# Seven query groups in the first round, four pixel chunks summed by GpSimd, and three more GELU chunks on VectorE

## The chip, the cores and the metric

The kernel runs on one core of a Trainium2 chip. The metric is the device time of one execution in microseconds; the kernel before takes 950.07 us, the median of three runs (949.9 to 951.19). Engines are named as in the profile: PE (TensorE, matmuls), ACT (ScalarE), DVE (VectorE), POOL (GpSimd), SP (SyncE, which here only issues transfers).

## The reference

Four batches of 12288 queries of 128 channels attend to keys that are made from pooled pixels; keys and values are the same matrix. What comes out goes through a two-layer network of width 2048.

```python
B, C, H, W = 4, 128, 384, 32                       # q: (B, H*W, C); kv: (B, H, W, C)
kv_pool = kv.reshape(B, H // 4, 4, W // 4, 4, C).mean(axis=(2, 4))
k = v = kv_pool.reshape(B, -1, C) @ w_sr           # 768 keys per batch
s = (q @ k.transpose(0, 2, 1)) / np.sqrt(C)
a = softmax(s)                                     # over the keys
x = (a @ v).reshape(B * H * W, C)
h = x @ w_in                                       # d_ff = 2048
out = (h * (1.0 / (1.0 + np.exp(-1.702 * h)))) @ w_out
```

## The kernel before

**Tiling.** A group is 512 queries; there are 96 groups, 24 a batch. For a group the scores are six chunks of 128 keys by 512 queries, and the network has 16 chunks of 128 hidden units by 512 tokens. A chunk is *filled* by one matmul of 512 columns into PSUM (L347 for scores, L593 for the network), taken by ACT with the exponential (L349) or GELU (L595) into one of 102 slots of the tile `ag`, and *drained* by matmuls from there: four of 129 columns for scores (L360: values and a column of ones for the sum), one of 512 for the network (L603). ACT takes one, two or three chunks in one instruction; PSUM has two areas of three banks for that, and the other banks serve sums of drains and small jobs (`acc`).

**Stages.** There are two rounds of 48 groups (batches 0 and 1, then 2 and 3): all scores of the round, then all of its network. At the start of the first round nothing is there, so the scores of the first six groups are taken key chunk by key chunk, as pixels land: `chunks` lists (group, key chunk), first groups 0 and 1 with two key chunks, then groups 2 to 5 with two, then each further key chunk for all six groups, then the remaining groups one by one.

**Keys of batches 0 and 1.** A pixel chunk is 128 partitions by 2048 numbers (16 pixels of 128 channels in a partition). `load_chunk` loads it with GpSimd's queue, casting float32 to bfloat16. `pool_chunk` sums four rows and four columns of pixels with 16 matmuls of 32 columns (L139: pixels as weights, `sum4` as the moving matrix), DVE copies the result (L142), `key_and_value` multiplies by `w_sr` both ways (L161, L162) and DVE copies keys and values (L163, L164). Batches 2 and 3 are summed by adding transfers, which the change leaves alone.

**Queries.** The first three query blocks (12 groups) are loaded by `load_q` and transposed on PE (`transpose_q`, L233); the others are cast to bfloat16 in DRAM by GpSimd's queue (`cast_q`) and brought in by a transposing transfer of SP's queue (`load_qT`). The attention's result is stored by `put_away` and brought back transposed by `bring_back`, both on SP's queue.

**What sets the order.** Each engine takes its instructions in the order in which the program is written. That order comes from a small model that runs while the program is built: `now` counts PE time in units of one 512-column matmul, `end` holds when ACT will be done with each instruction, `dve` when DVE will be done, `COST` and `COPY` what small jobs cost on PE and DVE. Fills go ahead of ACT by two; between them drains are put as long as the next fill is not held up; `extras` are small jobs that wait for a free spot, and `first` names jobs that stand ahead of a certain fill. `background(i)` starts loads and jobs when group i is first filled; `gate` makes GpSimd's queue wait until DVE has come to that place.

**Chunks that DVE takes.** DVE computes the exponential of 32 chunks and the GELU of some network chunks of the second round (`lent`, `lent_gelu`: 13 elementwise operations and two reciprocals), so that ACT has less to do. `RECIPROCAL` is the model's price of one such reciprocal.

Of the kernel before, what the change touches and what calls it, by code (L numbers as in the profile page):

```python
# [24 lines left out]
def kernel(  # L25
    ctx, tc, q, kv, w_sr, moe_w_in, moe_w_out, out,
):
    nc = tc.nc
    B, N, C = q.shape
    _, H, W, _ = kv.shape  # L30
    r = 4
    Hp, Wp = H // r, W // r
    J = Hp * Wp
    JC = J // 128
    d_ff = moe_w_in.shape[1]
    FCH = d_ff // 128
    scale = 1.0 / (C ** 0.5)
    G = 512
    SG = 4 * G
    NG = B * N // G  # L40
    NS = NG // 4
    GB = NG // B
# [10 lines left out]
    kv_r = kv.rearrange("b (ch p) (a w) c -> b a ch p (w c)", p=128, a=2)  # L53
# [6 lines left out]
    XS = NS // R  # L60
# [7 lines left out]
    kvtmp = ctx.enter_context(tc.tile_pool(name="kvtmp", bufs=1))  # L68
# [51 lines left out]
    def new_keys(b):  # L120
        kTs[b] = kvres.tile([128, J], BF, name="kT")

        vs[b] = kvres.tile([128, JC, C + 8], BF, name="v")
        nc.vector.memset(vs[b][:, :, C:C + 1], 1.0)

    def load_chunk(b, jc):

        a, ch = divmod(jc, HC)
        t = x_tile(XS - 1 - jc)
        nc.gpsimd.dma_start(out=t, in_=kv_r[b, a, ch])  # L130
        kv_tiles[b, jc] = t.rearrange("p (wp w1 c) -> p w1 wp c", w1=r, c=C)

    def pool_chunk(b, jc):
# [7 lines left out]
        pTs[b, jc] = kvtmp.tile([128, 128], BF, name="pTc", bufs=2)  # L141
        nc.vector.tensor_copy(pTs[b, jc], ps[:, 0:128])  # L142

    def key_chunk(b, jc):
        if jc == 0:
            new_keys(b)
        ps = acc()
        nc.tensor.matmul(ps[:, 0:128], w_sr_sb, pTs[b, jc], start=True, stop=True)
        nc.vector.tensor_copy(kTs[b][:, jc * 128:jc * 128 + 128], ps[:, 0:128])
# [5 lines left out]
        vs[b, jc] = True  # L155

    def key_and_value(b, jc):
        if (b, jc) == (1, 0):
            new_keys(b)
        ps = acc()  # L160
        nc.tensor.matmul(ps[:, 0:128], w_sr_sb, pTs[b, jc], start=True, stop=True)  # L161
        nc.tensor.matmul(ps[:, 128:256], pTs.pop((b, jc)), w_sr_sb, start=True, stop=True)  # L162
        nc.vector.tensor_copy(kTs[b][:, jc * 128:jc * 128 + 128], ps[:, 0:128])  # L163
        nc.vector.tensor_copy(vs[b][:, jc, 0:C], ps[:, 128:256])  # L164
        vs[b, jc] = True
# [55 lines left out]
    def load_q(s, lo, hi):  # L221
        nc.gpsimd.dma_start(  # L222
            out=qs[s].rearrange("p (g e) -> p g e", g=4)[:, lo:hi, :],
            in_=q_flat[s * SG + lo * G:s * SG + hi * G, :].rearrange("(g p i) c -> p g (i c)", p=128, i=4))
# [22 lines left out]
    load_chunk(0, 1)  # L247
    load_q(0, 2, 4)
    load_q(1, 0, 2)
    for jc in range(2, JC):  # L250
        load_chunk(0, jc)
    load_q(1, 2, 4)
    for s in range(2, QS):
        load_q(s, 0, 2)
        load_q(s, 2, 4)
    cast_q(3)
    cast_q(4)

# [67 lines left out]

    early = range(NG // R, NG // R + EARLY)
    rolling = [(i, JC - 1) for i in [*range(38, NG // R, 6), *range(57, 90, 6)]]
    lent = [(g, FCH - 1) for g in range(52, 94, 3)]
    aside = agpool.tile([128, K, 512], BF, name="aside")  # L330

    def weights(c):
# [161 lines left out]
    PART, FIRST = 24, 3  # L494

    def put_away(n, m):
        size = PART // 2 if n == 0 and m > FIRST + 1 else PART
        for o in range(m * PART, m * PART + PART, size):
            lo = n * XS * SG + o * T
            nc.sync.dma_start(out=x_bf[lo:lo + size * T, :].rearrange("(k p) c -> p k c", p=T),  # L500
                              in_=x[:, o * T:(o + size) * T].rearrange("p (k c) -> p k c", k=size))
# [22 lines left out]
    def background(i):  # L524

        first_round = i < GB * 2
        s = TURN.get(i, NS) if first_round else i // 4 + 3 if i % 4 == 0 else NS
        if s < NS:
            load_qT(s)
        if i in CAST:  # L530
            gate()
            for s in CAST[i]:
                cast_q(s)
        if i in (10, 12):
            gate()
            for jc in range(i % 10 * 3 // 2, i % 10 * 3 // 2 + 3):
                load_chunk(1, jc)
        if 0 <= i - 16 < JC:
            extras.append((key_and_value, 1, i - 16))
        if 0 <= i - 15 < JC:  # L540
            extras.append((pool_chunk, 1, i - 15))
        if i in (28, 33, 38):
            put_away(0, (i - 28) // 5)
        if i in (31, 36, 41):
            bring_back(0, (i - 31) // 5)
        if i == 27:
            gate()
# [98 lines left out]
    NA, NM = NG * JC, NG * FCH  # L646
    chunks, sizes = [], [1] * 2 + [2] * 28
    chunks += [(0, 0), (1, 0), (0, 1), (1, 1)]
    chunks += [(i, jc) for i in range(2, 6) for jc in range(2)]
    chunks += [(i, jc) for jc in range(2, JC) for i in range(6)]  # L650
    chunks += [(i, jc) for i in range(6, NG) for jc in range(JC) if i not in early and (i, jc) not in rolling]
    seq, todo = [], []
    todo_early = [("a", t, a) for t in range(NT) for a in range(2) if (t // TS * TS + TS - 1) // 4 in early]
    for n in range(R):
# [39 lines left out]
    def later(g):  # L694
        extras.append((transpose_q, g))

    def jobs(p):

        nonlocal now
        for f, *args in first.get(p, ()):  # L700
            if f in COST:
                now = max(now, free[next_acc()])
            f(*args)
            if f in COST:
                now += COST[f][0]
                free[last_acc] = copied(f)

    def prepare(p):

        nonlocal now  # L710
        kind, part = seq[p]
        for i, jc in part:
            if (kind, i) not in begun:
                begun.add((kind, i))
                (background if kind == "a" else background_moe)(i)
            while kind == "a" and ((key_and_value, i // GB, jc) in extras or (transpose_q, i) in extras):
                f, *args = extras.pop(0)
                now = max(now, free[next_acc()]) + COST[f][0]
                f(*args)
                free[last_acc] = copied(f)  # L720

    first = {
        0: [(pool_chunk, 0, 0), (transpose_q, 0), (warm, 1), (key_chunk, 0, 0), (transpose_q, 1)],
        1: [(value_chunk, 0, 0), (warm, 1)],
        2: [(pool_chunk, 0, 1), (warm, 2), (key_and_value, 0, 1), (warm, 1), (transpose_q, 2)],
        3: [(transpose_q, 3)],
        4: [(transpose_q, 4)],
        5: [(transpose_q, 5)],
        6: [(pool_chunk, 0, 2)],
        7: [(key_and_value, 0, 2)],  # L730
        9: [(pool_chunk, 0, 3)],
        10: [(key_and_value, 0, 3)],
        12: [(pool_chunk, 0, 4)],
        13: [(key_and_value, 0, 4)],
        15: [(pool_chunk, 0, 5)],
        16: [(key_and_value, 0, 5), (later, 6)],
        17: [(later, 7)],
        18: [(later, g) for g in range(8, 12)]}

    FIXED, CHUNK, SWITCH, HANDOVER, EVACUATE = 0.295, 1.978, 6.0, 1.0, 4.5
    COST = {pool_chunk: (1.9, 2.6), key_chunk: (0.3, 2.4), value_chunk: (0.3, 2.4),
            transpose_q: (1.05, 4.2), early_fill: (1.0, 5.5), key_and_value: (0.55, 3.5),
            transpose_pooled: (0.9, 3.6), make_k: (0.8, 3.2), make_v: (0.8, 3.7)}
    COPY = {pool_chunk: 1.5, key_chunk: 1.5, value_chunk: 1.5, key_and_value: 2.8, transpose_q: 3.2}
    SMALL = 0.26
    RECIPROCAL = 10.5
    PAUSE = 4.0  # L750
    end, extra_at = [], 0.0
    source, dve = None, 0.0
# [7 lines left out]
    def copied(f):  # L760
        if f not in COPY:
            return now + COST[f][1]
        on_dve(COPY[f])
        return max(now + COST[f][1], dve)

    def fill(p):
        nonlocal now
        if p >= len(seq):
            return
        kind, part = seq[p]  # L770
        prepare(p)
        if p == 4:
            turns.insert(0, 2)
        if p == narrow - 5:
            for m in (2, 5):
                turns.remove(m)
        if p == narrow:
            assert not any(m in closes for m in (2, 5))
            now = max(now, free.pop(2), free.pop(5))
        lo = K * (p % 2)  # L780
        (fill_attn if kind == "a" else fill_moe)(part, banks[:, lo:lo + len(part), :])
        if p >= 2:
            now = max(now, end[p - 2] + HANDOVER / 2)
        now += len(part)
        begin = max(now + HANDOVER / 2, end[p - 1] if p else 0.0)
        if p and kind != seq[p - 1][0]:
            begin += SWITCH
        end.append(begin + FIXED + CHUNK * len(part))
# [101 lines left out]
```

The softmax here doesn't subtract the row's maximum and nothing guards it: scores larger than these inputs give would overflow.

## Time and profile before

Busy time of the engines in the profiled execution, which spans 948.6 us:

| engine | busy us | instructions |
|---|---|---|
| PE | 941.8 | 6314 |
| ACT | 934.9 | 710 |
| DVE | 536.5 | 1035 |
| POOL | 66.5 | 114 |

| transfers | number | KB each | us from issue to landing (median) |
|---|---|---|---|
| pixels, GpSimd's queue (L130) | 11 | 512 | 10.4 |
| pixels, SP's queue (L242) | 1 | 1024 | 5.1 |
| queries for PE transposes (L222) | 5 and 2 | 256 and 128 | 15.5 and 5.5 |
| queries cast in DRAM (L209) | 21 | 512 | 6.9 |

ACT does 502 GELU instructions of three chunks, 8 of two; 162 exponentials of three chunks, 28 of two and 2 of one. The first exponential starts at 8.69 us; the third, which needs the second pixel chunk, at 12.28. A row of a group gives line, engine, operation, what is written and read, the count, then busy time and the mean duration, then the idle time of that engine just ahead and who ended it. Busy times of pipelined instructions overlap, so time between starts is what one costs.

### The profile page before, as it was taken

What the parts mean: (1) busy time and instruction counts of PE and PEld (TensorE: products, weight loads), DVE (VectorE), ACT (ScalarE), POOL (GpSimd) and SP (SyncE); (2) the same over time, 40 slices, a digit from 0 to 9 for tenths busy, and PEclk for the clock granted to TensorE, in tenths of its full rate; (3) what the DMA queues carried; (4) which work ended last, traced back from release to release, by engine and by line L of the source; (5) the groups of instructions that cost most, each with busy time, mean ns of one, the idle gap of its engine ahead of it and who ended that gap; (6) DMA issues with size and microseconds to landing.
All of it is one profiled execution on the core that took longest, in us unless ns stands there. A gap on an engine that the chain in (4) does not pass through costs nothing.

```text
span 948.6 us, 15423 instructions
## 1 busy us (share of the span) xinstructions
PE 941.8 (99%) x6314; PEld 502.9 (53%) x6314; DVE 536.5 (57%) x1035; ACT 934.9 (99%) x710; POOL 66.5 (7%) x114
## 2 busy tenths in 40 slices
PE   8999999999999999999999999999999999999998
PEld 4677776444444444454446777754444444444444
DVE  4643653102577777778655765365666665566631
ACT  6999999999999999999999999999999999999998
POOL 3101001320000232000000000000000000000000
PEclk9999999999999999999999999999999999999999
DMA  9999922999767799864335583562222222222222
GB/s 209 209 170 193 206 64 45 158 125 180 153 130 115 113 154 119 123 103 79 64 55 113 134 161 76 133 122 36 43 35 44 34 46 34 45 33 45 34 45 45
DMA packets 372855, 95.46 MB, mean 101 GB/s; under 512 B 346720, under 2 KB 370400, under 8 KB 372320
## 3 DMA queue, kind: packets, MB, share of 16 engines
q1 hardware_dynamic: 344000, 62.36, 36.9%
q0 software_dynamic: 28512, 31.99, 22.3%
q8 instruction: 49, 0.80, 0.4%
q14 instruction: 22, 0.18, 0.1%
q10 hardware_dynamic: 272, 0.13, 0.0%
HBM read 52.49 MB, written 48.76 MB: 107 GB/s over the span
## 4 chain that ended last, share of the span: by engine, by line
ACT 88%; PE 9%; DMA 2%; issue 0%; DVE 0%; POOL 0%; POOLq 0%
ACT ag L595 71%; ACT ag L349 17%; PE banks L347 4%; PE banks L360 3%; DMA qT<-q_bf 1%; DMA x<-in_kv_dram 1%; PE banks L139 0%; PE banks L593 0%; PE banks L631 0%; ACT L595 0%; PE banks L603 0%; PE banks L233 0%; ACT L349 0%; DVE kT L163 0%; POOL x L222 0%
## 5 line engine op out<-in xcount | busy, mean ns | idle before, releaser
L595 ACT ACTIVATE ag<-banks 128x1536 bf16<-128x1536 f32 (+1 forms) x510 | 682.2, 1507 | 0.0
L593 PE MATMUL banks<-x,w_in_sb 128*128 128x512 bf16 x1522 | 411.7, 379 | 0.1
L603 PE MATMUL banks<-ag,w_out_sb 128*128 128x512 bf16 x1506 | 407.8, 379 | 0.0
L349 ACT ACTIVATE ag<-banks 128x1536 bf16<-128x1536 f32 (+2 forms) x192 | 245.8, 1439 | 3.8 <-PE banks L347 3.4
L603 PEld LDWEIGHTS <-w_out_sb 128*128 128x128 bf16 x1520 | 148.4, 98 | 178.1 <-issue 0.9
L593 PEld LDWEIGHTS <-w_in_sb 128*128 128x128 bf16 x1522 | 147.3, 98 | 170.4 <-issue 1.1
L614 DVE STREAM_TRANSPOSE o_sb<-banks 128x512 f32<-128x512 f32 x95 | 67.9, 715 | 210.7 <-PE banks L603 195.0
L360 PEld LDWEIGHTS <-ag 128*128 128x128 bf16 x2272 | 146.1, 98 | 46.4 <-issue 0.6
L360 PE MATMUL banks<-v,ag 128*128 128x129 bf16 x2272 | 163.7, 220 | 0.1
L347 PE MATMUL banks<-qT,kT 128*128 128x512 bf16 x544 | 148.7, 379 | 1.6 <-DVE kT L163 1.0
L439 DVE SCALAR_TENSOR_TENSOR ea<-ea,eb 128x512 f32<-128x512 f32 x128 | 87.9, 687 | 3.2
L383 DVE RECIPROCAL rec<-banks 128x3 f32<-128x3 f32 x124 | 22.3, 180 | 95.9 <-PE banks L360 95.9
L386 DVE TENSOR_TENSOR x<-banks,rec 128x384 bf16<-128x384 f32 x124 | 69.1, 558 | 4.3
L347 PEld LDWEIGHTS <-kT 128*128 128x128 bf16 x544 | 46.3, 98 | 26.5 <-DVE kT L163 1.7
L470 DVE RECIPROCAL eb<-ea 128x256 f32<-128x256 f32 x28 | 47.6, 1727 | 0.5
L173 POOL DMA_DIRECT2D kvs<-in_kv_dram x32 | 40.4, 1299 | 17.8 <-DMA kvs<-in_kv_dram 15.2
L428 DVE TENSOR_SCALAR ea<-banks 128x512 f32<-128x512 f32 x32 | 22.1, 692 | 32.8 <-PE banks L412 32.5
L463 DVE SCALAR_TENSOR_TENSOR ea<-ea,eb 128x512 f32<-128x512 f32 x56 | 38.3, 685 | 1.6
L518 POOL MEMSET gate_tile<- 1x1 f32 x37 | 3.9, 105 | 326.6 <-DVE gate_tile L517 326.6
L434 DVE SCALAR_TENSOR_TENSOR eb<-eb,ea 128x512 f32<-128x512 f32 x32 | 22.1, 690 | 0.9
L450 DVE TENSOR_SCALAR qT<-banks 128x512 f32<-128x512 f32 x14 | 9.7, 692 | 17.2 <-PE banks L406 16.9
L441 DVE SCALAR_TENSOR_TENSOR ag<-ea,ee 128x512 bf16<-128x512 f32 x24 | 16.5, 688 | 0.7
(83 smaller groups left out, 267.9 us busy)
## 6 DMA issues: line engine op xcount, KB each, us to landing
out_dram<-o_sb SPq DMA_DIRECT2D x380, 64.0 KB, 2.0
kvs<-in_kv_dram POOLq DMA_DIRECT2D x32, 384.0 KB, 6.3
q_bf<-in_q_dram POOLq DMA_DIRECT2D x21, 512.0 KB, 6.9
x_bf<-x SPq DMA_DIRECT2D x13, 768.0 KB, 5.8
x<-in_kv_dram POOLq DMA_DIRECT2D x11, 512.0 KB, 10.4
x_bf<-x SPq DMA_DIRECT2D x6, 384.0 KB, 4.6
x<-in_q_dram POOLq DMA_DIRECT2D x5, 256.0 KB, 15.5
x<-in_kv_dram SPq DMA_DIRECT2D x1, 1024.0 KB, 5.1
```

The lines of the kernel that those rows point to most:

```text
L173: nc.gpsimd.dma_start(out=kv_sums[b][:, i2], in_=kv_p[b, i, w, :, i2], **({"accum_op": ADD} if n else {}))
L347: nc.tensor.matmul(ps[:, k, :], kTs[i // GB][:, jc * 128:(jc + 1) * 128], rhs, start=True, stop=True)
L349: nc.scalar.activation(place([("a",) + c for c in chunks]), ps, AF.Exp, scale=scale)
L360: nc.tensor.matmul(av_of[u][:, k * (C + 1):(k + 1) * (C + 1)], weights(("a", i, jc))[:, o:o + T], vs[i // GB][:, jc, 0:C + 1], start=(jc = ...
L386: nc.vector.tensor_tensor(to, ps[:, :, 0:C], rec.unsqueeze(2).broadcast_to([128, TS, C]), MUL)
L439: nc.vector.scalar_tensor_tensor(a, a, COEFFS[k], b, ADD, MUL)
L463: nc.vector.scalar_tensor_tensor(a, a, COEFFS[k], b, ADD, MUL)
L470: nc.vector.reciprocal(b[:, m:m + 256], a[:, m:m + 256])
L593: nc.tensor.matmul(ps[:, k, :], w_in_sb[:, fc * 128:(fc + 1) * 128], x[:, g % (4 * XS) * G:(g % (4 * XS) + 1) * G], start=True, stop=True)
L595: nc.scalar.activation(place([("m",) + c for c in chunks]), ps, AF.Gelu_apprx_sigmoid)
L603: nc.tensor.matmul(o_of[g], w_out_sb[:, fc, :], weights(("m", g, fc)), start=(fc == 0), stop=(fc == FCH - 1))
L614: nc.vector.transpose(o_sb, o_of.pop(g))
```

## The change

Five parts:

1. The first round takes seven groups key chunk by key chunk instead of six. Loads are reordered for it: half of block 1's second part comes ahead of pixel chunks 2 to 5, the other half behind. One warm-up matmul is dropped ahead of `transpose_q(2)`.
2. The model of the order gets landings (`LAND`, in its units) and times at which keys and queries are ready (`ready`), so that it knows when PE would stand and waits.
3. Of the second batch's six pixel chunks, four are loaded as float32 by SP's queue, two at a time into the same two places, and summed over the four columns by GpSimd (three adds each); two are cast by GpSimd's loads as before. Pooling and keys of this batch go in pairs of chunks.
4. `lent` has 17 chunks instead of 14, two and three groups apart in turn; `RECIPROCAL` falls from 10.5 to 8.2.
5. `put_away` of the first round stores in halves from its second part on, instead of its last ones alone.

The aim is less work for ACT (4), less for PE (3), and an order of the first round that stands less (1, 2).

```diff
+    SUMS = 4
+    held, sums = {}, {}
+
+    def load_pixels(jc):
+        a, ch = divmod(jc, HC)
+        o = (XS - 4 + jc % 2 * 2) * SG
+        t = x[:, o:o + 2 * SG].bitcast(F32)
+        if jc < 2:
+            nc.vector.memset(t[:, 0:1], 0.0)
+        nc.sync.dma_start(out=t, in_=kv_r[1, a, ch])
+        kv_tiles[1, jc] = t.rearrange("p (wp w1 c) -> p w1 wp c", w1=r, c=C)
+
+    def sum_pixels(jc):
+        t = kv_tiles.pop((1, jc))
+        if jc % 2 == 0:
+            held[jc // 2] = opool.tile([128, 512], F32, name="o_sb").bitcast(BF)
+        sums[jc] = held[jc // 2][:, jc % 2 * 512:jc % 2 * 512 + 512].rearrange("p (wp c) -> p wp c", c=C)
+        nc.gpsimd.tensor_tensor(t[:, 0], t[:, 0], t[:, 1], ADD)
+        nc.gpsimd.tensor_tensor(t[:, 2], t[:, 2], t[:, 3], ADD)
+        nc.gpsimd.tensor_tensor(sums[jc], t[:, 0], t[:, 2], ADD)
+
+    def pool_pair(b, jc):
+        ps = acc()
+        for k in range(2):
+            t = None if jc + k in sums else kv_tiles.pop((b, jc + k))
+            for wp in range(4):
+                o = k * 128 + 32 * wp
+                parts = [t[:, w, wp, :] for w in range(r)] if t is not None else [sums[jc + k][:, wp, :]]
+                for w, part in enumerate(parts):
+                    nc.tensor.matmul(ps[:, o:o + 32], part, sum4, start=(w == 0), stop=(w == len(parts) - 1))
+        pTs[b, jc] = kvtmp.tile([128, 256], BF, name="pTp")
+        nc.vector.tensor_copy(pTs[b, jc], ps[:, 0:256])
...
-    for jc in range(2, JC):
-        load_chunk(0, jc)
-    load_q(1, 2, 4)
-    for s in range(2, QS):
-        load_q(s, 0, 2)
-        load_q(s, 2, 4)
+    load_q(1, 2, 3)
+    load_chunk(0, 2)
+    load_chunk(0, 3)
+    load_chunk(0, 4)
+    load_chunk(0, 5)
+    load_q(1, 3, 4)
+    load_q(2, 0, 2)
+    load_q(2, 2, 4)
...
-    lent = [(g, FCH - 1) for g in range(52, 94, 3)]
+    lent = [(g, FCH - 1) for g in range(52, 94) if g % 5 in (2, 4)]
...
-        size = PART // 2 if n == 0 and m > FIRST + 1 else PART
+        size = PART // 2 if n == 0 and m > 0 else PART
...
-        if i in (10, 12):
+        if i == 10:
             gate()
-            for jc in range(i % 10 * 3 // 2, i % 10 * 3 // 2 + 3):
+            for jc in range(2):
+                load_pixels(jc)
+            for jc in range(SUMS, JC):
                 load_chunk(1, jc)
-        if 0 <= i - 16 < JC:
-            extras.append((key_and_value, 1, i - 16))
-        if 0 <= i - 15 < JC:
-            extras.append((pool_chunk, 1, i - 15))
+        if 0 <= i - 11 < SUMS:
+            sum_pixels(i - 11)
+            if i - 9 < SUMS:
+                load_pixels(i - 9)
+        for at_, jc in ((17, 0), (19, 4), (21, 2)):
+            if i == at_:
+                extras.append((pool_sums if jc < SUMS else pool_pair, 1, jc))
+            if i == at_ + 1:
+                extras.append((key_pair, 1, jc))
...
-    chunks += [(i, jc) for i in range(2, 6) for jc in range(2)]
-    chunks += [(i, jc) for jc in range(2, JC) for i in range(6)]
+    chunks += [(i, jc) for i in range(2, 7) for jc in range(2)]
+    chunks += [(i, jc) for jc in range(2, JC) for i in range(7)]
...
+        now = max(now, free[next_acc()], LAND.get((f, *args), 0.0), ready.get((f, *args), 0.0))
+        f(*args)
+        now += COST[f][0]
+        free[last_acc] = copied(f)
...
-        2: [(pool_chunk, 0, 1), (warm, 2), (key_and_value, 0, 1), (warm, 1), (transpose_q, 2)],
+        2: [(pool_chunk, 0, 1), (warm, 2), (key_and_value, 0, 1), (transpose_q, 2)],
...
-    RECIPROCAL = 10.5
+    RECIPROCAL = 8.2
...
+    LAND = {(transpose_q, 0): 0.9, (transpose_q, 1): 3.8, (pool_chunk, 0, 1): 15.1, (transpose_q, 2): 21.0, (transpose_q, 3): 21.0, (transpose_q, 4): 26.9, (transpose_q, 5): 26.9, (transpose_q, 6): 29.8, (pool_chunk, 0, 2): 41.1, (pool_chunk, 0, 3): 52.5, (pool_chunk, 0, 4): 67.5, (pool_chunk, 0, 5): 78.8, (transpose_q, 7): 81.7, (transpose_q, 8): 87.6, (transpose_q, 9): 87.6, (transpose_q, 10): 93.5, (transpose_q, 11): 93.5}
+    ready = {}
...
+        if kind == "a":
+            now = max(now, *[ready.get(("k", i // GB, jc), 0.0) for i, jc in part], *[ready.get(("q", i), 0.0) for i, jc in part])
```

The jobs that `first` names move by one fill accordingly: group 6's transpose stands ahead of fill 6, pooling and keys of pixel chunks 2 to 5 ahead of fills 7, 8, 10, 11, 14, 15, 17 and 18.

More of the change, by code (lines that the diff above doesn't have):

```diff
@@ L142, in pool_chunk, with pool_sums, key_pair @@
         nc.vector.tensor_copy(pTs[b, jc], ps[:, 0:128])
+    SUMS = 4
[27 more added lines that the diff above has]
+        nc.vector.tensor_copy(pTs[b, jc], ps[:, 0:256])
+    def pool_sums(b, jc):
+        pool_pair(b, jc)
+    def key_pair(b, jc):
+        if not any(k == (b, m) for k in vs for m in range(JC)):
+            new_keys(b)
+        ps = acc()
+        pT = pTs.pop((b, jc))
+        nc.tensor.matmul(ps[:, 0:256], w_sr_sb, pT, start=True, stop=True)
+        for k in range(2):
+            nc.tensor.matmul(ps[:, 256 + k * 128:384 + k * 128], pT[:, k * 128:(k + 1) * 128], w_sr_sb,
+                             start=True, stop=True)
+        nc.vector.tensor_copy(kTs[b][:, jc * 128:(jc + 2) * 128], ps[:, 0:256])
+        nc.vector.tensor_copy(vs[b][:, jc:jc + 2, 0:C], ps[:, 256:512].rearrange("p (k c) -> p k c", k=2))
+        vs[b, jc] = vs[b, jc + 1] = True
     def key_chunk(b, jc):
@@ L157, in key_and_value @@
     def key_and_value(b, jc):
-        if (b, jc) == (1, 0):
-            new_keys(b)
         ps = acc()
@@ L648 @@
     chunks += [(0, 0), (1, 0), (0, 1), (1, 1)]
-    chunks += [(i, jc) for i in range(2, 6) for jc in range(2)]
-    chunks += [(i, jc) for jc in range(2, JC) for i in range(6)]
-    chunks += [(i, jc) for i in range(6, NG) for jc in range(JC) if i not in early and (i, jc) not in rolling]
+    chunks += [(i, jc) for i in range(2, 7) for jc in range(2)]
+    chunks += [(i, jc) for jc in range(2, JC) for i in range(7)]
+    chunks += [(i, jc) for i in range(7, NG) for jc in range(JC) if i not in early and (i, jc) not in rolling]
     seq, todo = [], []
@@ L695, in later, with job @@
         extras.append((transpose_q, g))
+    def job(f, args):
+        nonlocal now
+        if f not in COST:
+            now += args[0] if f is warm else 0.0
+            f(*args)
+            return
+        now = max(now, free[next_acc()], LAND.get((f, *args), 0.0), ready.get((f, *args), 0.0))
+        f(*args)
+        now += COST[f][0]
+        free[last_acc] = copied(f)
+        if f is pool_chunk:
+            for then in (key_chunk, value_chunk, key_and_value):
+                ready[(then, *args)] = free[last_acc]
+        if f in (key_chunk, key_and_value):
+            ready[("k", *args)] = free[last_acc] - (1.0 if f is key_and_value else 0.0)
+        if f is transpose_q:
+            ready["q", args[0]] = free[last_acc]
     def jobs(p):
-        nonlocal now
         for f, *args in first.get(p, ()):
[L701 to L706, printed above, removed]
+            job(f, args)
     def prepare(p):
@@ L715, in prepare @@
                 (background if kind == "a" else background_moe)(i)
-            while kind == "a" and ((key_and_value, i // GB, jc) in extras or (transpose_q, i) in extras):
+            while kind == "a" and ((key_pair, i // GB, jc // 2 * 2) in extras or (transpose_q, i) in extras):
                 f, *args = extras.pop(0)
-                now = max(now, free[next_acc()]) + COST[f][0]
-                f(*args)
-                free[last_acc] = copied(f)
+                job(f, args)
     first = {
@@ L728 @@
         5: [(transpose_q, 5)],
[L729 to L738, printed above, removed]
+        6: [(transpose_q, 6)],
+        7: [(pool_chunk, 0, 2)],
+        8: [(key_and_value, 0, 2)],
+        10: [(pool_chunk, 0, 3)],
+        11: [(key_and_value, 0, 3)],
+        14: [(pool_chunk, 0, 4)],
+        15: [(key_and_value, 0, 4)],
+        17: [(pool_chunk, 0, 5)],
+        18: [(key_and_value, 0, 5), (later, 7)],
+        19: [(later, 8)],
+        20: [(later, 9), (later, 10), (later, 11)]}
     FIXED, CHUNK, SWITCH, HANDOVER, EVACUATE = 0.295, 1.978, 6.0, 1.0, 4.5
-    COST = {pool_chunk: (1.9, 2.6), key_chunk: (0.3, 2.4), value_chunk: (0.3, 2.4),
+    COST = {pool_chunk: (1.9, 2.6), pool_sums: (1.1, 3.2), pool_pair: (3.8, 3.2), key_pair: (1.1, 5.0), key_chunk: (0.3, 2.4), value_chunk: (0.3, 2.4),
             transpose_q: (1.05, 4.2), early_fill: (1.0, 5.5), key_and_value: (0.55, 3.5),
             transpose_pooled: (0.9, 3.6), make_k: (0.8, 3.2), make_v: (0.8, 3.7)}
-    COPY = {pool_chunk: 1.5, key_chunk: 1.5, value_chunk: 1.5, key_and_value: 2.8, transpose_q: 3.2}
+    COPY = {pool_chunk: 1.5, pool_sums: 2.1, pool_pair: 2.1, key_pair: 4.2, key_chunk: 1.5, value_chunk: 1.5, key_and_value: 2.8, transpose_q: 3.2}
     SMALL = 0.26
-    RECIPROCAL = 10.5
+    RECIPROCAL = 8.2
     PAUSE = 4.0
```

## Prediction

> **What bounds the kernel now.** I read the page first, then ACT's groups by form, then PE and ACT in order of time, then busy time by stage, then the waits.
>
> ```profile
> PE 941.8 (99%) x6314; PEld 502.9 (53%) x6314; DVE 536.5 (57%) x1035; ACT 934.9 (99%) x710; POOL 66.5 (7%) x114
> ...
> ACT 88%; PE 9%; DMA 2%; issue 0%; DVE 0%; POOL 0%; POOLq 0%
> ```
>
> Two engines are busy for 99%. The chain that ended last is ACT for 88%, but that alone does not say that PE has room, so I look at the stages (us of the window, then busy us of PE, weight loads, DVE, ACT, GpSimd).
>
> ```profile
> 12.28:38.00 25.72, 24.30 (x259) 15.19 (x257) 17.04 (x44) 25.55 (x28) 1.68 (x5) 1.00 1.09 211
> 38.00:142.00 104.00, 103.54 (x1220) 75.66 (x1219) 50.87 (x150) 103.45 (x78) 9.07 (x23) 1.00 0.88 163
> 142.00:487.00 345.00, 345.00 (x1820) 165.32 (x1818) 196.99 (x366) 344.99 (x257) 48.03 (x70) 1.00 0.78 116
> 604.00:936.00 332.00, 332.00 (x1663) 155.61 (x1662) 191.67 (x276) 331.97 (x248) 0.00 (x0) 1.00 0.29 48
> 936.00:948.60 12.60, 9.35 (x89) 5.88 (x87) 1.52 (x4) 7.99 (x10) 0.00 (x0) 1.00 0.32 59
> ```
>
> From 12.28 us on ACT is idle for some 0.8 us until 936. In 604 to 936 there are 1663 matmuls in 332 us, 0.200 us each, some nine in ten of them 512 wide; a 512-wide matmul starts some 0.214 us after the one ahead (in the timeline below, three of L347 from 52.51, the next operation at 53.15), so PE has no gap there either, and works off drains that lie behind. The two engines are balanced: the end comes from whichever has more left. A gain needs both to be shortened.
>
> ACT's price of one instruction in the last stage, and its only idle spots in the first:
>
> ```profile
> L595 ACT ACTIVATE ag<-banks 128x1536 bf16<-128x1536 f32 x246 | 330.8, 1480 | 0.0
> ```
>
> ```profile
> 12.28 88.65 ACT L349 ACTIVATE ag<-banks 128x1024 bf16<-128x1024 f32 x74 [2.30 <-PE banks L347]
> 101.36 29.78 ACT L349 ACTIVATE ag<-banks 128x1536 bf16<-128x1536 f32 x22 [0.42 <-PE banks L347]
> ```
>
> The first column of the group is the union: 330.8 / 246 = 1.345 us per instruction of three chunks; the mean of 1.480 overlaps. The wait of 2.30 us before 12.28 hangs on the landing of the second pixel chunk.
>
> PE around the second batch's pooling, and what PE waits for in the whole run:
>
> ```profile
> 52.10 0.55 PE L139 MATMUL banks<-sum,x 128*128 128x32 bf16 x16
> 52.51 0.81 PE L347 MATMUL banks<-qT,kT 128*128 128x512 bf16 x3
> ...
> 54.53 0.22 PE L162 MATMUL banks<-w_sr_sb,pTc 128*128 128x128 bf16 x1
> 54.86 0.67 PE L360 MATMUL banks<-v,ag 128*128 128x129 bf16 x9
> ```
>
> ```profile
> PE banks L347 <- DVE kT L163: 1.0, 4, 0.4
> ...
> PE banks L412 <- DMA qT<-q_bf: 0.4, 1, 0.4
> ```
>
> A pooled chunk holds PE 52.51 - 52.10 = 0.41 us for 16 matmuls (0.025 us each). After the first key matmuls of the batch PE stands from 54.53 to 54.86, 0.33 us where 0.06 would do.
>
> **What the Trainium skill says.** "Trainium Kernel Development and Optimization", Performance Expectations: matmul busy time is a bad metric, as matmuls are pipelined. The trace agrees (L347 shows a mean of 0.379 us a matmul, but starts are 0.214 apart), so I count PE by starts. "GPSIMD Engine Reference", 3.1: a float32 `tensor_tensor` add of 2048 columns took 4.497 us there; no GpSimd add is in this trace. "DMA: Bandwidth & Descriptors", Anatomy of one DMA: about 2.0 us plus bytes / 436e3, written for GpSimd's loads, so for 1 MB an estimate of 4.4 us; this trace's one 1024 KB pixel load, from SP, took 5.1 us beside others.
>
> **The change part by part.**
>
> *17 GELU chunks instead of 14 on DVE.* The second round's list falls from 754 to 751 chunks; eight two-chunk instructions stay at its end, so exactly one three-chunk instruction goes: ACT -1.345 us. PE still makes the same matmuls. DVE pays: a chunk has 8 operations of about 0.69, 5 of about 0.43 and two reciprocals of 1.727 us, so about 11.1 us busy and, with the transposes that come between, some 14 us from first to last. DVE's 191.67 us of 332 become 225, 68%. The chunks stand 2 and 3 groups apart instead of 3; a group takes about 6.85 us, so two jobs of 14 us have 34 us. They fit, with little room in the shorter gap: 0 to +0.4 us on PE if a group's drain has to wait.
>
> *Four chunks of the second batch summed on GpSimd, pooling and keys in pairs.* PE now: 6 x 0.41 = 2.46 us. After: a summed chunk takes 4 matmuls, not 16, so 4 x 0.10 + 2 x 0.41 = 1.22 us. PE -1.24. Keys in pairs: 256 + 2 x 128 columns for a pair, the same columns as before: 0. The stall of 0.27 us behind the first key is three operations of DVE before the copy; with half as many handovers I take it away: PE -0.27, and of ACT's late starts at 52.10, 56.21 and 60.46 (together 0.47 us over their 1.33 us beat) some 0.3. DVE copies the same columns in half the instructions: off the path.
>
> GpSimd: 512 columns of the page's add are an estimate of 4.497 / 4 = 1.1 us; low end the DVE row of 0.69 us, high end double, 2.3 us, for contention. Three adds, the third waiting on two: about 3.7 us a chunk, 15 in all. Is it in time? Group 10's background fires at 37.8 us (where GpSimd's gate stands now), and a group lasts two instructions of 1.33, 2.66 us. Two pixel loads of 1 MB and two casting loads share the queues (2.45 us per MB by today's landings, 45.47, 47.92, 50.39): first pixels in by 45, second by about 49. Sums done at 49 and 53; they are used by group 17's job, 37.8 + 7 x 2.66 = 56.4. Loads three and four wait for sums one and two, land by 53 and 57; sums at 57 and 61, used at group 21, 67. Spare 3 and 6 us. Behind the waiting adds in GpSimd's queue stand the casts of query blocks 6, 7 and 8 (46.72, 48.39 and 52.37 now): they go out at 53, 57 and 61 and take some 5; their transposes start at 65.35, 68.18 and 71.75. Hidden, but only just. Behind the waiting pixel loads in SP's queue nothing stands until 65.35. So 0.
>
> *First round with seven groups; loads in another order; one warm-up matmul less.* The second pixel chunk still lands at 9.80, since nothing ahead of it is moved, so ACT's start at 12.28 stays but for the dropped warm-up: the transposes ran at 11.42 behind it, the fill at 11.65, and the key copy (11.20 plus 0.3) would allow it at 11.5: -0.1 on both. Chunks three to six land about 0.6 us later (256 KB of queries go ahead), but each is needed 0.9 us later or more: the four waits on kT (1.0 us) stay, as the order of pool, key and fill around them is the same. The first drain needs the third pixel chunk for groups 0 and 1, one two-chunk instruction (0.905 us) later than now; PE has nothing else then, so it may lose 0.3 to 0.9 us, which a better view of landings may give back, since the writer of the order now knows when PE would stand. I take 0 net, range -1.0 to +0.9.
>
> *Smaller stores at put_away; RECIPROCAL 8.2.* The unit of the order is one matmul, so 8.2 is 1.77 us, close to the 1.727 measured; 10.5 was 2.27. It only lets DVE's jobs be put closer. Halved stores may let the query transpose that landed at 100.07 in sooner: ACT's late start there (0.55 us over its beat) halves or stays: ACT -0.2.
>
> **Sum.** ACT: -1.345 - 0.1 - 0.3 - 0.2 = -1.95. PE: -1.24 - 0.27 - 0.1, and 0.27 us at 936.44, where PE waits for ACT and which it need not any more: -1.9. So both get about 1.9 to 2.0 shorter: 950.07 - 1.95 = 948.1 us.
>
> **Rivals.** (a) PE becomes the bound: the first round's later drains cost the 0.3 to 0.9, the stall behind the first key comes back (0.27), the longer DVE jobs cost 0.2: PE gets -1.0 at most, 949.1, no change that can be told. For it: PE is full to the end already. Against it: the four kT waits have some slack to give. (b) GpSimd's adds take double, or DVE's accesses hold them up: sums of 7 us each end at 52, 59, 66 and 73, so PE stands some 2.5 us at 56.4 and up to 6 at 67, with ACT behind it; less the gain, 950.6 to 954, likely 952. For it: nothing in this trace shows the price. Against it: the margin at the page's price. (c) The denser GELU jobs finish late and hold the drains of their groups, 17 times 0.15 us: 950.6. Against it: DVE waits 106 us for o in that stage now. (d) The order with landings also removes the early stalls (ACT's late starts up to 142 us come to 1.9 us over the beat): -3.0, 947.0.
>
> **How the numbers follow.** Main case 0.40, (a) 0.27, (b) 0.12, (c) 0.07, (d) 0.14. Main and (d) are faster by over 0.2% (under 948.17), but the main case lies on the edge, so of its 0.40 I give 0.10 to no change; (a) is no change but for 0.05. Faster 0.46, same 0.34, slower 0.20. Range: (d) down to 946.6; up to 951.0, which leaves the worse half of (b) out.
>
> **What would show it.** L595 three-chunk instructions 501 instead of 502; ACT's first two-chunk instruction at about 12.2; the second batch's pooling with 48 matmuls instead of 96; GpSimd's adds near 1.1 us and done before the sums' matmuls, with no wait of PE on GpSimd; PE's waits on kT still about four. Wrong if PE waits for GpSimd, if gaps appear on PE in 604 to 936, or if the first drain moves by more than 1 us.

## The result, and the profile after

The changed kernel takes 957.11 us (median of six executions, 953.34 to 958.05) where the kernel before takes 950.28: a ratio of 1.0063, with a 95% interval of 1.0044 to 1.0081. It is slower by 6.8 us; 948.1 was predicted. The profiled execution, spanning 951.5 us, is the shortest of the six, and shows only part of the loss; the trace of a longer one stands among the experiments.

The page's busy times and the chain of the changed kernel:

```profile
PE 940.9 (99%) x6262; PEld 501.9 (53%) x6262; DVE 569.2 (60%) x1072; ACT 933.5 (98%) x709; POOL 79.3 (8%) x122
...
PE 54%; ACT 43%; DMA 2%; DVE 0%; issue 0%; POOL 0%; POOLq 0%
```

ACT has one instruction less (709). PE has 52 matmuls less (6262): 48 in the pooling, three in the keys taken in pairs, one warm-up, as the working had it. But the chain that ended last has gone over: it was ACT for 88%, now PE has more than half of it, and ACT's wait at the very end, for what PE still has to do, grew from 1.3 to 3.3 us. PE sets the end.

By stage (us of the window, then busy us of PE, weight loads, DVE, ACT, GpSimd, the granted clock):

```profile
100.00:104.00 4.00, 2.49 (x22) 1.55 (x23) 2.00 (x5) 1.38 (x2) 0.00 (x0) 1.00 0.87 190
604.00:936.00 332.00, 332.00 (x1679) 156.32 (x1678) 224.69 (x323) 331.97 (x248) 0.00 (x0) 1.00 0.29 48
936.00:951.50 15.50, 11.69 (x99) 6.85 (x97) 2.24 (x5) 8.60 (x10) 0.00 (x0) 0.97 0.29 52
```

Two things are to be seen. In 604 to 936 PE is full, as before: the denser GELU jobs of DVE (224.69 us busy, 225 predicted) leave no gap. Around 100 us PE and ACT both stand (2.49 and 1.38 us busy of 4). ACT's three-chunk GELU instructions in the last stage, and ACT in order of time:

```profile
L654 ACT ACTIVATE ag<-banks 128x1536 bf16<-128x1536 f32 x245 | 329.5, 1475 | 0.0
```

```profile
12.27 87.86 ACT L401 ACTIVATE ag<-banks 128x1024 bf16<-128x1024 f32 x74 [2.30 <-PE banks L399]
102.75 40.75 ACT L401 ACTIVATE ag<-banks 128x1536 bf16<-128x1536 f32 x30 [2.62 <-PE banks L399]
```

329.5 / 245 is 1.345 us an instruction, the same price. The wait of 0.42 us that stood at 101.36 is 2.62 us at 102.75. PE in order of time shows for what, first the kernel before, then the changed one:

```profile
100.12 0.39 PE L412 MATMUL banks<-qT,kT 128*128 128x512 bf16 x1 [0.36 <-DMA qT<-q_bf]
```

```profile
97.82 0.81 PE L399 MATMUL banks<-qT,kT 128*128 128x512 bf16 x3
101.51 0.39 PE L464 MATMUL banks<-qT,kT 128*128 128x512 bf16 x1 [2.88 <-DMA qT<-q_bf]
101.73 0.33 PE L412 MATMUL banks<-v,ag 128*128 128x129 bf16 x3
```

L464 (L412 before) is the matmul of `early_fill`, which writes the fill and DVE's exponential of a chunk that DVE takes, here chunk 5 of group 38. It needs query block 9, which a transposing transfer brings. It stands behind the 196th score matmul in both kernels. PE comes there at 98.6 now, instead of some 99.8, and the block lands at 101.46 instead of 100.07. So of the 2.5 us by which the stand grew, 1.1 come from PE's being earlier and 1.4 from the later landing. Behind L464 in PE's queue wait the drains, which need nothing of block 9, and the next fills, for which ACT waits. The transfer in SP's queue, before and after:

```profile
92.36 5.04 SPq L215 DMA_TRANSPOSE qT<-q_bf  x1
```

```profile
91.74 5.10 SPq L265 DMA_TRANSPOSE qT<-q_bf  x1
```

It was issued 0.6 us earlier than before and landed 1.4 us later.

The second batch's pooling, and PE's waits in the whole run:

```profile
56.72 0.35 PE L176 MATMUL banks<-sum,o_sb 128*128 128x32 bf16 x8
56.92 0.50 PE L412 MATMUL banks<-v,ag 128*128 128x129 bf16 x6
```

```profile
PE banks L464 <- DMA qT<-q_bf: 2.9, 1, 2.9
...
PE banks L399 <- DVE kT L213: 0.6, 2, 0.4
```

A pair of summed chunks holds PE 56.92 - 56.72 = 0.20 us, as worked out. PE has no wait for GpSimd in the list and none behind the first key of the batch. The four waits on kT are two.

### The profile page after: what moved, and what is told of

Read it like the earlier page. It is cut to its first block, busy times and chain, and to the rows that moved or that the text cites. A ratio compares the mean times of both kernels' runs of the same rounds, so it can differ in the third digit from the quotient of the medians.

```text
span 951.5 us, 15386 instructions
## 1 busy us (share of the span) xinstructions
PE 940.9 (99%) x6262; PEld 501.9 (53%) x6262; DVE 569.2 (60%) x1072; ACT 933.5 (98%) x709; POOL 79.3 (8%) x122
## 4 chain that ended last, share of the span: by engine, by line
PE 54%; ACT 43%; DMA 2%; DVE 0%; issue 0%; POOL 0%; POOLq 0%
ACT ag L654 35%; PE banks L662 18%; PE banks L652 18%; ACT ag L401 9%; PE banks L412 9%; PE banks L399 8%; DMA qT<-q_bf 1%; DMA x<-in_kv_dram 1%; PE banks L464 1%; PE banks L690 0%; ACT L654 0%; POOL x L272 0%; PE banks L176 0%; PE banks L283 0%; DVE o_sb L673 0%
## 5 line engine op out<-in xcount | busy, mean ns | idle before, releaser
L412 PEld LDWEIGHTS <-ag 128*128 128x128 bf16 x2272 | 146.2, 98 | 46.7 <-issue 0.9
L412 PE MATMUL banks<-v,ag 128*128 128x129 bf16 x2272 | 163.8, 220 | 0.0
L491 DVE SCALAR_TENSOR_TENSOR ea<-ea,eb 128x512 f32<-128x512 f32 x128 | 87.8, 686 | 3.5 <-issue 0.3
L522 DVE RECIPROCAL eb<-ea 128x256 f32<-128x256 f32 x34 | 57.6, 1722 | 0.5
L515 DVE SCALAR_TENSOR_TENSOR ea<-ea,eb 128x512 f32<-128x512 f32 x68 | 46.6, 685 | 2.0
L502 DVE TENSOR_SCALAR qT<-banks 128x512 f32<-128x512 f32 x17 | 11.8, 692 | 21.6 <-PE banks L458 21.4
```

Source lines behind the costliest of these rows:

```text
L412: nc.tensor.matmul(av_of[u][:, k * (C + 1):(k + 1) * (C + 1)], weights(("a", i, jc))[:, o:o + T], vs[i // GB][:, jc, 0:C + 1], start=(jc = ...
L491: nc.vector.scalar_tensor_tensor(a, a, COEFFS[k], b, ADD, MUL)
L515: nc.vector.scalar_tensor_tensor(a, a, COEFFS[k], b, ADD, MUL)
L522: nc.vector.reciprocal(b[:, m:m + 256], a[:, m:m + 256])
```

## The experiments

Theory: the loss is PE's stand for block 9, made longer by a clock that falls after a long stand, and the rest of the change is a gain that PE's losses in the first round eat. Rivals: the stand only moves an idle time that comes anyway; the denser GELU jobs; the seven groups themselves. All times are medians, each with the ratio to the kernel before on the same chip and its 95% interval.

### The stand at group 38

Held back to a later place in PE's queue (called the guard below):

```diff
-  return (i // GB, jc) in vs and i // 4 - 1 <= group // 4 and len(used) > rolling.index((i, jc)) - K
+  return (i // GB, jc) in vs and i // 4 - 1 <= group // 4 and len(used) > rolling.index((i, jc)) - K and (i != 38 or group >= 34)
```

> The changed kernel, with the exponential that DVE takes for group 38 held back until group 34 is being filled (it went out at group 32). Theory 1, the loss is PE standing 2.9 us at about 98.5 for query block 9's transposing transfer, and the granted clock that falls after so long a stand (means of 0.996 to 0.998 in five of six executions): the wait is gone, the clock is 1.000 in every execution, and the time is about 953.3 - 2.9 = 950.4 us, since PE ends the run and gets all of it back. Rival, the first round's order or the denser GELU jobs lose the time and this wait only moves an idle time that would come anyway: 955 or more, with new gaps on PE.

Measured: 950.08 us, ratio 0.9999 (0.9991 to 1.0007). The wait is gone from PE's list and the time is what was expected. The mean clock is 1.000 in eleven of thirteen executions, not in all: 0.999 in one and 0.998 in another, the longest (951.77 us), of which there is no trace. So one matmul in the wrong place of PE's queue explains the whole loss, 7.0 us of the changed kernel's time, and with it gone the change is no gain either.

With the matmul where it was, and the two weight loads eight groups later:

```diff
-  if i == 27:    # w_in_sb
+  if i == 35:
...
-  if i == 28:    # w_out_sb
+  if i == 36:
```

> The changed kernel, with the two loads of the network's weights started at groups 35 and 36 instead of 27 and 28; the order of PE, ACT and DVE is otherwise as it was. Theory 1 with the cause in the transfers: block 9's transposing transfer has no casting loads beside it and lands 3 to 5 us earlier than 101.5, PE's wait falls under 0.5 us, 950.4 us. Rival, the transfer is late by itself (issued at 91.7, it takes 9 us whatever is beside it): the wait stays 2.5 to 3 us and the time at 953 to 957.

Measured: 950.67 us, ratio 1.0005 (0.9997 to 1.0013). SP's queue in order of time:

```profile
91.85 1.77 SPq L265 DMA_TRANSPOSE qT<-q_bf  x1
```

The transfer holds SP's queue 1.77 us instead of 5.10, lands at 96.26, and PE has no wait there. The place in the queue does no harm by itself; together with a block that lands late beside the weight loads, it does.

### Why most executions lost more than the profiled one

> The changed kernel once more, for a trace of an execution like most of its own. In five of six executions it took 955.6 to 958.1 us with a mean clock of 0.996 to 0.998, and in the profiled one 953.3. Theory 1: query block 9 lands later than 101.5 here (102 to 103.5), PE stands 4 to 5 us, and the clock's row shows half speed for some microseconds after it, a loss of 2 to 3.5 us more. Rival, the clock falls elsewhere: the stand is 2.9 us as before, and matmuls are slow in another stage.

Measured: 956.02 us for the one execution. By stage, with the granted clock as the third number from the end:

```profile
98.00:103.00 5.00, 0.50 (x3) 0.00 (x1) 0.00 (x0) 2.00 (x2) 0.00 (x0) 1.00 1.43 122
103.00:106.00 3.00, 2.95 (x16) 1.85 (x17) 2.10 (x5) 0.70 (x1) 0.00 (x0) 0.50 1.18 238
106.00:110.00 4.00, 3.95 (x44) 2.94 (x43) 2.06 (x6) 3.52 (x4) 0.00 (x0) 0.95 1.04 248
```

```profile
103.05 0.61 PE L464 MATMUL banks<-qT,kT 128*128 128x512 bf16 x1 [4.55 <-DMA qT<-q_bf]
103.45 0.53 PE L412 MATMUL banks<-v,ag 128*128 128x129 bf16 x3
103.77 1.49 PE L399 MATMUL banks<-qT,kT 128*128 128x512 bf16 x3
```

The block landed at 103.00, PE stood 4.55 us, and for 3.4 us afterwards the clock was at half: three matmuls of 512 columns from 103.77 to 105.05, 0.43 us each. So a landing 1.5 us later costs 1.5 us of stand and half of 3.4 us more, 3.2 together by this working; the execution is 2.7 us longer than the profiled one, so part of it was won back later. The means of 0.996 in other executions would be some 7.6 us at half speed, an estimate (0.004 of 955 us, twice); no trace shows one of these. The Trainium skill, "TensorE: Matmul & The Clock Gate", Part 1, has the rule: the clock is halved after an idle window of about 3.4 us and comes back after a busy one, and the windows run freely. The runs agree, with a stand of 2.88 us that left the clock alone, one of 4.55 that did not, and 3.4 us at half; a second stand of 4.54 us, in the last experiment below, was followed by 3.4 us at half as well.

The stand filled with work:

```diff
+  if i == 38:
+      for _ in range(13):
+          nc.tensor.matmul(ps[:32, :], ones, ones.unsqueeze(1).broadcast_to([128, 16, 32]), start=True, stop=True)
   nc.tensor.matmul(ps, kTs[i // GB][:, jc * 128:(jc + 1) * 128], rhs, start=True, stop=True)
```

> The changed kernel with 13 additional matmuls of 512 columns (2.8 us, their result is overwritten) right ahead of group 38's early matmul, where PE stands. They need no transfer, so they fill the stand and the landing stays at about 101.5. Theory 1 with the clock: PE is not idle, so the granted clock stays at 1.000 in every execution and the time is that of the one execution without a fallen clock, about 953.3 us. Rival, the clock falls for another cause: means of 0.996 to 0.998 as before, 957 us or, with the additional work, 958.

Measured: 954.95 us, ratio 1.0052 (1.0040 to 1.0065), and a mean clock of 1.000 in four of five executions; the fifth, the longest (956.65 us), had 0.998. PE in the profiled execution:

```profile
98.47 2.98 PE L466 MATMUL banks<-ones 128*32 128x512 bf16 x13
103.41 0.38 PE L467 MATMUL banks<-qT,kT 128*128 128x512 bf16 x1 [1.96 <-DMA qT<-q_bf]
```

The block landed at 103.37, not 101.5, so PE was busy for 2.98 us with the additional matmuls and stood another 1.96. That is a longer hold-up than the 4.55 us of the run above, and it still took 1.1 us less: with PE at work through most of it, the clock did not fall. The expected time was missed because the landing is not fixed; the part on the clock held in four executions of five.

### The parts alone

The 17 GELU chunks, put into the kernel before:

```diff
-  lent = [(g, FCH - 1) for g in range(52, 94, 3)]
+  lent = [(g, FCH - 1) for g in range(52, 94) if g % 5 in (2, 4)]
...
-  RECIPROCAL = 10.5
+  RECIPROCAL = 8.2
```

> The kernel before with only the 17 GELU chunks on DVE and RECIPROCAL 8.2. If PE is what sets the end there (it has no gap from 26 us on), ACT's 1.345 us bring nothing but what PE waited for at the end, 0.27 us: 949.8 to 950.3. If ACT sets the end: 948.7. If the denser DVE jobs hold drains up: over 950.6, with gaps on PE in 604 to 936.

Measured: 950.52 us, ratio 1.0005 (0.9997 to 1.0014): between the cases that were expected, and no difference that can be told from none. ACT's wait at the end, in the list of ACT's waits, grew from 1.3 us to

```profile
ACT o_sb L639 <- DMA out_dram<-o_sb: 2.9, 1, 2.9
```

ACT stood 1.6 us longer for PE at the end (the line names a transfer of an output tile; in the fastest version below the same wait is put down to PE's last drains, L690). The drains that PE has behind it are the same, so ACT's 1.345 us are worth nothing alone.

The pooling, and then pooling and GELU chunks together, with the guard and the first round as it was (the core of the pooling's diff):

```diff
-        if i in (10, 12):
+        if i == 10:
...
+            for jc in range(2):
+                load_pixels(jc)
...
+            sum_pixels(i - 11)
...
+                extras.append((pool_sums if jc < SUMS else pool_pair, 1, jc))
...
+                extras.append((key_pair, 1, jc))
```

> The kernel before with only the second batch's pooling changed (four chunks summed by GpSimd, pairs), group 38's exponential held back. PE makes 48 matmuls less (1.24 us) and loses its stand of 0.27 us, ACT has as much as before. If the two engines are balanced, ACT now sets the end and only its own late starts of 0.3 us come off: 949.6 to 950.1. If PE alone sets the end: 948.8.

> The kernel before with the pooling in pairs and the 17 GELU chunks together, the first round as it was, group 38's exponential held back. Both engines get shorter, PE by 1.24 and 0.27, ACT by 1.345 and 0.3: 948.6 to 949.0, less than either part alone brings. Rival, PE's 1.24 us do not reach the end because its drains are held by something else: 950 as with the guard alone.

Measured: 949.48 us, ratio 0.9989 (0.9983 to 0.9996), and 948.98 us, ratio 0.9986 (0.9979 to 0.9993). Since both have the guard, they need a control, the kernel before with the guard alone (the first edit above):

> The kernel before with only group 38's exponential held back to group 34, a control for the runs that hold it back. PE's wait of 0.4 us there goes: 949.9 to 950.3. If holding it back costs something of its own (DVE's later chunks shift): 950.6 or more, and the runs with it have to be read with that.

Measured: 949.69 us, ratio 0.9991 (0.9984 to 0.9997), better than expected: the kernel before gains 0.7 us from not standing at group 38. The changed kernel with the guard, 950.08 us, is no better than that. Against the control, the pooling brings 0.2 us, which lies within the intervals, and both parts 0.7: 13 of the 17 executions with both lie below the lowest of the control's 21. The pooling alone leaves the end to ACT (ACT waits only 0.6 us at the end, 1.3 in the control, and PE waits 0.5 us for ACT there), and the GELU chunks alone leave it to PE. So the engines are balanced, and both have to be shortened. Both together are still a smaller gain than the 1.5 us of PE and 1.65 of ACT that were worked out: ACT then waits 1.7 us at the end, so it is PE again that has more left. Where PE loses the rest is not shown.

The first round alone, with the guard:

```diff
-    chunks += [(i, jc) for i in range(2, 6) for jc in range(2)]
-    chunks += [(i, jc) for jc in range(2, JC) for i in range(6)]
+    chunks += [(i, jc) for i in range(2, 7) for jc in range(2)]
+    chunks += [(i, jc) for jc in range(2, JC) for i in range(7)]
...
+        now = max(now, free[next_acc()], LAND.get((f, *args), 0.0), ready.get((f, *args), 0.0))
```

> The kernel before with only the first round changed (seven groups, order of loads, landings in the model, one warm-up less), group 38's exponential held back as in the run with the guard. PE keeps the pooling's 1.24 us and stands 0.9 us more for ACT before 28 us: 950.7 to 951.2. Rival, the new first round is a gain of its own: 949.5 or less.

Measured: 951.93 us, ratio 1.0015 (1.0008 to 1.0021): 2.2 us over the control, more than expected. Drain matmuls on PE between 12.28 and 38 us, first the kernel before, then this one, then the same without the model:

```profile
L360 PE MATMUL banks<-v,ag 128*128 128x129 bf16 x96 | 8.4, 220 | 0.0
```

```profile
L414 PE MATMUL banks<-v,ag 128*128 128x129 bf16 x76 | 6.9, 220 | 0.1
```

```profile
L414 PE MATMUL banks<-v,ag 128*128 128x129 bf16 x94 | 8.2, 220 | 0.1
```

The last is this run, which takes only the model of landings and ready keys out again:

```diff
-  now = max(now, free[next_acc()], LAND.get((f, *args), 0.0), ready.get((f, *args), 0.0))
+  now = max(now, free[next_acc()])
...
-  if kind == "a":
-      now = max(now, *[ready.get(("k", i // GB, jc), 0.0) for i, jc in part], *[ready.get(("q", i), 0.0) for i, jc in part])
```

> The run with the first round alone (951.93), without the model of landings and of ready keys; seven groups, order of loads and the dropped warm-up stay. In that run PE had done 76 drain matmuls by 38 us where the kernel before had done 96. If the model costs it (it lets PE count as late, so that no drain is put between fills): 90 or more drains by 38 us, 950.3 to 950.8. If the seven groups cost it (the first drain comes one instruction later and there is nothing else to do): 75 to 80 drains, 951.7 to 952.0.

Measured: 949.52 us, ratio 0.9988 (0.9982 to 0.9995), 2.4 us less than with the model, better than expected, and about the same as the control (949.69). What the model does stands in PE's order from 25 to 28 us, with it:

```profile
26.33 0.59 PE L401 MATMUL banks<-qT,kT 128*128 128x512 bf16 x2
27.25 0.59 PE L401 MATMUL banks<-qT,kT 128*128 128x512 bf16 x2 [0.32 <-ACT ag L403]
27.68 0.39 PE L285 MATMUL banks<-ident,x 128*128 128x128 bf16 x4
```

and without it:

```profile
26.16 0.59 PE L401 MATMUL banks<-qT,kT 128*128 128x512 bf16 x2
26.59 0.50 PE L414 MATMUL banks<-v,ag 128*128 128x129 bf16 x6
26.93 0.39 PE L285 MATMUL banks<-ident,x 128*128 128x128 bf16 x4
27.15 0.59 PE L401 MATMUL banks<-qT,kT 128*128 128x512 bf16 x2
```

The six drains at 26.59 have no place in the order with the model, and PE waits 0.32 us for ACT with nothing to do. By a reading of the code, the model raises `now`, the count of PE time, while `limit`, up to which drains are put ahead of a fill, hangs on ACT's count; with PE counted as late, there seems to be no room. With the model 20 drains of 0.057 us fewer are done by 38 us than in the kernel before (76 against 96), 1.1 us of PE, and 24 fewer by 60 us. That is about half of the 2.4 us. Another 0.6 us is a wait of PE for DVE at 487 us, which the run without the model doesn't have; the rest has not been followed up.

### The version that beats both

The whole change, with the guard and without the model (the first and the last of the diffs above):

> The whole change with group 38's exponential held back and without the model of landings and ready keys. If the model costs the drains: about 948.9, as the pooling in pairs and the GELU chunks give with six groups. If the seven groups do: 950.1, as the run with the guard alone.

Measured: 948.40 us, ratio 0.9981 (0.9975 to 0.9988): 2.0 us under the kernel before, 1.3 under the control with the guard alone, the fastest of all runs and better than expected. One of its 21 executions took 952.14 us, at a mean clock of 0.998; no trace shows why.

### What stays open

With early weights, block 9 lands at 101.5, 102.3, 103.0, 103.2, 103.4, 104.3 and 104.5 in the seven runs with the pixel sums (the expectation below says eight), and at 99.7, 99.8, 100.1, 100.3 and 100.4 in the five without. So the pixel part makes it late (the run with the pooling alone, 104.5, and its control, 100.4, differ in nothing else), though its last pixels land at 62. The halved stores of `put_away`, which were not run by themselves, are not the cause: 104.3 and 104.5 are the two runs of the pooling that store as before. The second weight load goes with it: 98.8 to 104.7 against 97.9 to 98.8. One suspect was tried in the fastest version, the casts that stand behind GpSimd's sums:

```diff
-  CAST = {0: [5], 13: [6], 14: [7], 15: [8], 25: [9, 10], 26: [11, 12]}
+  CAST = {0: [5], 11: [6], 12: [7], 13: [8], 25: [9, 10], 26: [11, 12]}
```

> The fastest run so far (the whole change, group 38's exponential held back, no model of landings; 948.40), with the casts of query blocks 6, 7 and 8 put into GpSimd's queue two groups earlier, so that at most one of the sums stands ahead of each. In all eight runs with the pixel sums and early weights block 9 lands at 101.5 to 104.5, in all five without them at 99.7 to 100.4. If the casts that stand behind the sums (issued at 54.8, 60.6 and 66.1 instead of 46.7, 48.4 and 52.4) push the later transfers back: block 9 lands at 100.5 or earlier again, the time is unchanged, 948.2 to 948.6. If it is something else of the pixel loads: 101.5 or later.

Measured: 953.34 us, ratio 1.0028 (1.0018 to 1.0038). It does not answer the question. A cast now went out beside the pixel loads, which landed later; the second sum was done at 61.3, and PE stood for it, which moved all that follows:

```profile
61.34 0.27 PE L176 MATMUL banks<-sum,o_sb 128*128 128x32 bf16 x4 [4.54 <-POOL gate_tile L570]
...
62.38 1.49 PE L399 MATMUL banks<-qT,kT 128*128 128x512 bf16 x3
```

(The profile names the GpSimd instruction next to the sum.) After this stand, too, three matmuls of 512 columns take 0.43 us each, from 62.38 to 63.66. Why the transfers near 100 us are slower with the pixel sums is open. What the run does show is how little room the sums have. In the fastest version the second sum was done at 56.0 and PE took it at 56.6; in the run with the pooling alone it was done at 57.0, and PE waited 0.2 us for it.

## Why the prediction was wrong, by its steps

**The step that failed first** is in part five: "ACT's late start there halves or stays: ACT -0.2". The 0.55 us at block 9's landing were taken as a leftover that could only shrink. I had named the transfer and its landing, and the view of PE's waits had the line of L412 waiting for it; but I did not ask what an earlier PE would meet there. The matmul's place in PE's queue is fixed, and the landing did not become earlier with PE: PE came 1.1 us earlier, the block 1.4 us later, with the pixel sums, and the wait of 0.36 us became 2.88 in the profiled execution and 4.55 in another. It cost 7.0 us (957.11 against 950.08), with the fall of the clock in it, for which the prediction had no term.

**The second** is in the first round: "I take 0 net, range -1.0 to +0.9". Rival (a) was right in that PE became the bound and that the first round's drains came later, but not about the reason. The seven groups by themselves are not slower (949.52 against the control's 949.69). The model of landings is, by 2.4 us alone and 1.7 in the whole change: I had expected it to give something back, "since the writer of the order now knows when PE would stand". It knew when PE would stand, and took its standing for work.

**What held.** ACT minus one instruction of 1.345 us; GpSimd's adds hidden; the pooling's 0.20 us for a pair of summed chunks; DVE's load in the last stage (224.69 us against 225), without a held drain; and that both engines have to be shortened together. Two smaller things did not hold. ACT's first two-chunk instruction started at 12.27, as before (12.28), so the 0.1 us of the dropped warm-up did not come. The waits on kT went from four to two, where I had said four; the first round does that, since both runs of the first round alone have two and both runs of the pooling with six groups have four. Without the two failing parts the time is 948.40, near the 948.1 of the main case, but that is in part luck: 0.7 of the 2.0 us is what the guard brings to the kernel before, and the parts of the change bring 1.3 where about 1.95 was worked out.

**The ranges.** Slower had 0.20, and rival (b) with 952 was the nearest in time, for another reason: PE did stand, but for a transfer and not for GpSimd. No rival had a stand that was already there and grew. The three chances do not follow from the shares given: 0.30 of the main case and 0.14 of (d) make 0.44 for faster, not 0.46, and (c), at 950.6, is no change by the 0.2% that was used.

**On the prices.** From the Trainium skill, "GPSIMD Engine Reference", 3.1, came the estimate of 1.1 us for an add of 512 columns. Here they took 1.26 us, and follow one another at 1.23 and 1.33:

```profile
46.40 1.26 POOL L163 TENSOR_TENSOR x<-x 128x512 f32<-128x512 f32 x1 [6.13 <-DMA x<-in_kv_dram]
47.63 1.26 POOL L164 TENSOR_TENSOR x<-x 128x512 f32<-128x512 f32 x1
48.96 1.27 POOL L165 TENSOR_TENSOR o_sb<-x 128x512 bf16<-128x512 f32 x1
```

Sums one and two were done at 50.2 and 54.8 (49 and 53 said) and used at 56.7: a spare of 1.9 us where I had 3. Sums three and four were done at 60.7 and 66.2 (57 and 61 said) and used at 67.3: a spare of 1.2 us where I had 6. The pixel loads took 7.3 us from issue to landing (median; the first one 38.98 to 46.26), not the 4.4 that were estimated for 1 MB from the Trainium skill, "DMA: Bandwidth & Descriptors", Anatomy of one DMA. Four loads were out together; that this is the reason was not tested.

## What to carry to other kernels

In a queue that runs in order, look at each wait that is near zero in the trace, and ask what happens to it when the engine comes earlier: if the other end is a transfer that does not land earlier too, the gain of all that was made faster ahead of it is lost there. Two engines that are both full gain only together; a change for one of them shows as nothing until the other is shortened. And a model that writes the order must count waiting apart from work, or a better count of time in it makes a worse order.

## What the hardware showed that I had not expected

A stand of PE can cost more than its length: one of 4.55 us was followed by 3.4 us in which a 512-wide matmul took 0.43 us instead of 0.214, up to 1.7 us more by that working. Filling 3.0 us of such a hold-up with matmuls that nobody needs was cheaper than leaving it idle (954.95 us for a hold-up of 4.9 us, against 956.02 in the one execution with a stand of 4.55). The same transfer, issued between 91.61 and 91.74, landed at 101.46, 103.00 and 103.37 in three runs whose order is the same up to there.
